# A last projection in half-width strips, and both halves of a query projection in one PSUM bank, in a two-part decode kernel

## The chip, the cores and the metric

One core of a Trainium2 chip. The metric is the device time of one execution in microseconds (us). The span is what the profile records, from the first to the last instruction; the timed number is 1.7 to 2.3 us more.

## The reference

Two attention layers decode one token, and their outputs are put side by side.

```
A: q = x @ wq                      x 1x512, wq 512x4096, 32 heads of 128
   p = softmax(q k^T / sqrt(128))  k, v: 32 heads x 32768 keys x 128, bf16
   a = (p v, heads side by side) @ wo        wo 4096x512
B: the same with 8 key/value heads, 4 query heads to each, last 4096 keys only
out = [a, b]                       1 x 1 x 1024
```

A alone reads 512 MiB of keys and values. The arithmetic is small beside that.

## The kernel before

SyncE queues loads deep ahead of their use. After the first query projection come B's attention, then 32 heads of A. The weights of the last projection, B's wo in two pieces and A's in five that shrink toward the end, are queued behind the last keys and values. So what follows the last byte is the rest of A's last projection and the store.

The query projection fills two banks, four strips of 512 in each:

```python
banks = (self.ACC, self.PT)
for tt in range(4):
    for b in range(2):
        for c in range(STRIPS):
            w = 4096 * tt + 512 * (4 * b + c)
            e.matmul(banks[b][32 * c:32 * c + 1, :], lhsT=t["x"][:, tt:tt + 1], rhs=wq[:, w:w + 512],
                     start=(tt == 0), stop=(tt == 3), tile_position=(0, 32 * c), ...)
# ... each bank cast to qrow by VectorE, then 8 small matmuls turn the rows into columns
```

The last projection: heads go in fours to four 32-column tiles of the array. B's pieces, and A's first three (heads 0 to 24), make four partial rows. VectorE copies these 128 partitions, and a float32 matmul with a column of ones folds them into two half rows. Then A's heads 25 to 31 are added in two half-width strips.

```python
WO_CUTS = {"A": (0, 11, 19, 25, 29, 32), "B": (0, 16, 32)}

def halves(self, e, bank, lhsT, rhs, begin, end):
    for i in range(2):
        e.matmul(bank[64 * i:64 * i + 1, 0:256], lhsT=lhsT, rhs=rhs[:, 256 * i:256 * i + 256],
                 start=begin, stop=end, tile_position=(0, 64 * i), ...)

for name, cut, bank, to in (("B", 2, self.S, self.ACC), ("A", 3, self.T[1], self.PT)):
    ...
    for part in range(cut):                      # four strips: bank[32 * (a % 4)]
        o = self.proj_part(name, part, ...)
    strips = dve(tensor_copy(self.pb[:, :], bank[:, :]), o, free)
    o = free = pe(self.halves(e, to, self.e32[:, 0:1], self.pb, True, whole), strips, ...)
    if whole:
        self.store("B", self.ACC, 512, o)
for part in range(3, 5):
    o = self.proj_part("A", part, ... self.halves(e, self.PT, lhsT, rhs, False, a == 31))
self.store("A", self.PT, 0, o)                   # cast, then a 1 KB store
```

## Time and profile before

| | before |
|---|---|
| time, median of the first 3 runs (range) | 1327.97 us (1327.24 to 1328.51) |
| the profiled run: time, span | 1328.94, 1327.2 us |
| DMA | 570.6 MB, 430 GB/s, one queue 99.6% of 16 engines' span |
| A's last wo piece lands | 1289.2 (issue) + 33.4 = 1322.6 us |
| from that landing to the end | 4.6 us |

From the page of the kernel before: TensorE's busy share and instructions, then busy tenths in 40 slices of the span, the granted TensorE clock in tenths of full speed, DMA, and the load queue's row.

```profile
PE 970.6 (73%) x13239; PEld 677.0 (51%) x13239; DVE 753.9 (57%) x1351; ACT 54.8 (4%) x167; POOL 2.2 (0%) x17
...
PEclk8886888887878888787888878788887878888797
DMA  9999999999999999999999999999999999999997
...
q1 hardware_dynamic: 13192, 570.44, 99.6%
```

No compute engine is full; DMA is. Only its last slice is thinner, and that slice holds the tail.

The chain of waits of the kernel before, its end: start, length, what.

```profile
1288.23 32.18 DMA kbuf<-in_A_wo_dram
1320.41 0.04 issue
1320.45 1.03 PE psT L742 x6
1321.48 0.02 issue
1321.51 0.70 DVE pb L745
1322.21 0.04 issue
1322.25 2.53 PE psPT L725 x18
1324.78 0.02 issue
1324.80 0.42 DVE out_sb L731
```

The last load in the chain is the third wo piece, not the fifth. The copy and the fold hold up the 14 matmuls of the last two pieces, which landed meanwhile. The matmuls of the tail in the timeline (start, length, operation, count, and in brackets the idle time before it and what ended it):

```profile
1316.06 0.81 PE L742 MATMUL psT<-kbuf,oz_A 128*1 128x512 bf16 x11 [1.13 <-DMA kbuf<-in_A_wo_dram]
1318.56 1.02 PE L742 MATMUL psT<-kbuf,oz_A 128*1 128x512 bf16 x8 [1.69 <-DMA kbuf<-in_A_wo_dram]
1320.45 1.02 PE L742 MATMUL psT<-kbuf,oz_A 128*1 128x512 bf16 x6 [0.87 <-DMA kbuf<-in_A_wo_dram]
...
1322.25 1.02 PE L725 MATMUL psPT<-pb,e 128*1 128x256 f32 x4 [0.79 <-DVE pb L745]
1323.06 1.71 PE L725 MATMUL psPT<-kbuf,oz_A 128*1 128x256 bf16 x14
```

Eleven matmuls took 0.81 us, the next eight 1.02 us. The windows view of the same stretch says why. Its columns are the stretch, its length, each engine's busy time (and count), and at the end the granted clock, the DMA share and GB/s.

```profile
1316.00:1318.00 2.00, 0.81 (x11) 0.19 (x11) 0.00 (x0) 0.00 (x0) 0.00 (x0) 0.87 1.00 411
1318.00:1320.00 2.00, 1.02 (x8) 0.10 (x8) 0.00 (x0) 0.00 (x0) 0.00 (x0) 0.50 0.99 390
1320.00:1322.00 2.00, 1.02 (x6) 0.10 (x6) 0.49 (x1) 0.00 (x0) 0.00 (x0) 0.50 0.42 149
1322.00:1324.00 2.00, 1.75 (x14) 0.85 (x16) 0.20 (x1) 0.00 (x0) 0.00 (x0) 0.50 0.01 0
```

The clock is at half from about 1317.5 us to the end of the work.

### The profile page before, as it was taken

What the parts mean: (1) busy time and instruction counts of PE and PEld (TensorE: products, weight loads), DVE (VectorE), ACT (ScalarE), POOL (GpSimd) and SP (SyncE); (2) the same over time, 40 slices, a digit from 0 to 9 for tenths busy, and PEclk for the clock granted to TensorE, in tenths of its full rate; (3) what the DMA queues carried; (4) which work ended last, traced back from release to release, by engine and by line L of the source; (5) the groups of instructions that cost most, each with busy time, mean ns of one, the idle gap of its engine ahead of it and who ended that gap; (6) DMA issues with size and microseconds to landing.
All of it is one profiled execution on the core that took longest, in us unless ns stands there. A gap on an engine that the chain in (4) does not pass through costs nothing. (4 is left out here: it accounts for less than half of the span.)

```text
span 1327.2 us, 28802 instructions
## 1 busy us (share of the span) xinstructions
PE 970.6 (73%) x13239; PEld 677.0 (51%) x13239; DVE 753.9 (57%) x1351; ACT 54.8 (4%) x167; POOL 2.2 (0%) x17
## 2 busy tenths in 40 slices
PE   4675678777777877767787776768777676877785
PEld 3463446555444655544465554446555444655552
DVE  4663556664555666455566645556664555666562
ACT  0000000000000000000000000000000000000000
POOL 0000000000000000000000000000000000000000
PEclk8886888887878888787888878788887878888797
DMA  9999999999999999999999999999999999999997
GB/s 402 429 436 426 442 429 440 427 440 431 425 440 431 440 427 438 433 429 437 433 440 425 440 431 429 438 431 440 425 438 433 429 437 433 440 425 438 433 429 330
DMA packets 13492, 570.60 MB, mean 430 GB/s; under 512 B 1828, under 2 KB 1832, under 8 KB 2216
## 3 DMA queue, kind: packets, MB, share of 16 engines
q1 hardware_dynamic: 13192, 570.44, 99.6%
q8 instruction: 8, 0.13, 0.0%
q10 hardware_dynamic: 288, 0.00, 0.0%
q14 instruction: 4, 0.03, 0.0%
HBM read 570.43 MB, written 0.00 MB: 430 GB/s over the span
## 5 line engine op out<-in xcount | busy, mean ns | idle before, releaser
L564 DVE COPY kt<-psT 128x1024 bf16<-128x1024 bf16 x1056 | 655.6, 683 | 235.7 <-PE psT L560 234.3
L560 PE MATMUL psT<-ident,kbuf 128*128 128x128 bf16 x8448 | 581.4, 235 | 165.4 <-DMA kbuf<-in_A_k_cache_dram 152.4
L560 PEld LDWEIGHTS psT<-ident,kbuf 128*128 128x128 bf16 x8448 | 541.8, 106 | 257.7 <-DMA kbuf<-in_A_k_cache_dram 160.5
L663 PE MATMUL psACC<-vbuf,ptsb 128*4 128x512 bf16 (+1 forms) x2112 | 187.6, 532 | 22.8 <-ACT ptsb L638 22.0
L583 PE MATMUL psS<-kt,qw 128*32 128x512 bf16 x2048 | 157.6, 385 | 14.9 <-DVE kt L564 14.9
L677 DVE TENSOR_SCALAR oc_A<-psACC,hot_A 128x128 f32<-128x128 f32 x32 | 11.2, 350 | 252.5 <-PE psG L690 252.5
L663 PEld LDWEIGHTS psACC<-vbuf,ptsb 128*4 128x4 bf16 (+1 forms) x2112 | 60.7, 111 | 140.1 <-issue 93.6
L611 ACT ACTIVATE psb<-psS,nb_A 128x512 bf16<-128x512 f32 x32 | 22.0, 687 | 1167.9 <-DVE nb_A L610 1167.9
L583 PEld LDWEIGHTS psS<-kt,qw 128*32 128x32 bf16 x2048 | 34.0, 95 | 57.6 <-DVE kt L564 30.7
L690 PE MATMUL psG<-oc_A,hw 128*32 128x128 f32 (+1 forms) x128 | 19.3, 227 | 52.3 <-DVE oc_A L679 52.3
L690 PEld LDWEIGHTS psG<-oc_A,hw 128*32 128x32 f32 x128 | 11.4, 109 | 62.4 <-DVE oc_A L679 55.0
L635 PE MATMUL psPT<-ident,psb 128*128 128x128 bf16 x136 | 18.3, 279 | 34.0 <-ACT psb L611 34.0
L679 DVE SCALAR_TENSOR_TENSOR oc_A<-psACC,hot_A,oc_A 128x128 f32<-128x128 f32 x96 | 33.6, 350 | 3.4
L600 DVE TENSOR_REDUCE tr_in<-psS 128x1 f32<-128x512 f32 x34 | 23.5, 692 | 17.1 <-PE psS L583 17.1
L635 PEld LDWEIGHTS psPT<-ident,psb 128*128 128x128 bf16 x136 | 10.4, 119 | 37.1 <-ACT psb L611 36.7
L604 PE MATMUL psACC<-rows,tr_in 128*1 128x64 f32 x64 | 8.7, 217 | 25.6 <-DVE tr_in L600 25.6
L638 ACT ACTIVATE ptsb<-psPT 128x512 bf16<-128x512 bf16 x34 | 20.3, 597 | 30.6 <-PE psPT L635 30.6
L604 PEld LDWEIGHTS psACC<-rows,tr_in 128*1 128x1 f32 x64 | 2.7, 81 | 35.1 <-DVE tr_in L600 35.1
L608 PE MATMUL psACC<-mr_A,nscale 1*128 1x1 f32 x64 | 12.1, 256 | 9.7 <-DVE mr_A L607 9.7
L608 PEld LDWEIGHTS psACC<-mr_A,nscale 1*128 1x128 f32 x64 | 9.4, 182 | 15.7 <-DVE mr_A L607 15.7
L610 DVE COPY nb_A<-psACC 128x1 f32<-128x1 f32 x32 | 5.1, 158 | 15.0 <-PE psACC L608 15.0
L607 DVE TENSOR_REDUCE mr_A<-psACC 1x1 f32<-1x64 f32 x32 | 6.8, 213 | 11.7 <-PE psACC L604 11.7
(85 smaller groups left out, 74.8 us busy)
## 6 DMA issues: line engine op xcount, KB each, us to landing
kbuf<-in_A_k_cache_dram SPq DMA_DIRECT2D x4, 4096.0 KB, 22.6
kbuf<-in_B_k_cache_dram SPq DMA_DIRECT2D x2, 4096.0 KB, 32.0
vbuf<-in_B_v_cache_dram SPq DMA_DIRECT2D x2, 4096.0 KB, 25.0
vbuf<-in_B_wq_dram SPq DMA_DIRECT2D x1, 4096.0 KB, 12.6
vbuf<-in_A_wq_dram SPq DMA_DIRECT2D x1, 4096.0 KB, 32.2
kbuf<-in_B_wo_dram SPq DMA_DIRECT2D x2, 2048.0 KB, 33.4
kbuf<-in_A_wo_dram SPq DMA_DIRECT2D x1, 1408.0 KB, 28.6
kbuf<-in_A_wo_dram SPq DMA_DIRECT2D x1, 1024.0 KB, 30.8
```

The lines of the kernel that those rows point to most:

```text
L560: inst = e.transpose(T[:, 128 * k:128 * k + 128], src[:, DH * k:DH * k + DH], self.ident[:, :])
L564: self.copies.append(self.op("dve", lambda v: v.tensor_copy(KT[:, :], T[:, :]), o, to="pe"))
L583: inst = e.matmul(self.S[32 * c:32 * c + 32, :], lhsT=win, rhs=self.kt[(bb + c // 2) % NKT][:, 512 * (c % 2):512 * (c % 2) + 512], start=b ...
L600: o = dve(lambda v: v.reduce_max(tr["in"][:, 0:1], self.S[:, :], axis=AXX), self.sdone, self.k_pool, to="pe" if name == "A" else None)
L604: o = self.op("pe", lambda e: e.matmul(self.ACC[0:1, 0:64], lhsT=tr["in"][:, 0:1], rhs=self.rows64[:, :], start=True, stop=True, skip_grou ...
L608: o = self.op("pe", lambda e: e.matmul(self.ACC[:, 64:65], lhsT=self.nscale[:, :], rhs=t["mr"][0:1, :], start=True, stop=True, skip_group_ ...
L611: self.sread = self.op("act", lambda s: s.activation(out=self.psb[:, :], in_=self.S[:, :], func=ACTF.Exp, bias=t["nb"][:, k:k + 1], scale= ...
L635: inst = e.transpose(PT[:, 128 * jj:128 * jj + 128], self.psb[:, 128 * jj:128 * jj + 128], self.ident[:, :])
L638: self.ptread = self.op("act", lambda s: s.activation(out=self.ptsb[:, :], in_=PT[:, 0:512], func=ACTF.Copy), self.psread, to="pe")
L663: inst = e.matmul(acc[32 * c:32 * c + rows, 0:512], lhsT=lhsT, rhs=rhs, start=begin, stop=end, tile_position=(0, 32 * c), skip_group_check ...
L679: o = self.op("dve", lambda v, src=src, hot=hot: v.scalar_tensor_tensor(out=oc, in0=src, scalar=hot, in1=oc, op0=ALU.mult, op1=ALU.add), p ...
L690: return self.op("pe", lambda e: e.matmul(self.G[0:32, c0 + c:c0 + c2], lhsT=win, rhs=t["oc"][g % len(t["oc"])][:, c:c2], start=False, sto ...
```

## The change

Its intent: take the copy and the fold off the end of A's projection, and take VectorE work out of the start. Three parts:

1. A's first wo piece (11 heads) runs as one full-width row. It is copied and folded in while later pieces land. Pieces 1 to 4 go straight into two half-width strips. B's rows are folded by one full-width float32 matmul.
2. Both halves of the query projection share one bank: x is stored between zeros, so a two-column window of it puts a half in row 0 or row 1 of a strip. One cast instead of two, four turning matmuls instead of eight.
3. Fewer VectorE steps for constants: some are built on GpSimd, four copies become one, one memset goes.

```diff
-                x=sb(f"x_{name}", [128, 4], BF16),
+                x=sb(f"x_{name}", [128, 12], BF16),
 ... (query projection)
+                    x = t["x"][:, 4 - 4 * b + tt:9 - 4 * b + tt:4]
-                        inst = e.matmul(banks[b][32 * c:32 * c + 1, :], lhsT=t["x"][:, tt:tt + 1], rhs=wq[:, w:w + 512],
-                                        start=(tt == 0), stop=(tt == 3), ...
+                        inst = e.matmul(acc[32 * c:32 * c + 2, :], lhsT=x, rhs=wq[:, w:w + 512], start=(tt == 0 and b == 0),
+                                        stop=(tt == 3 and b == 1), ...
-        for b in range(2):
-            o = self.op("dve", lambda v, b=b: v.tensor_copy(self.qrow[:, 512 * b:512 * b + 512], banks[b][:, :]), o)
+        self.accread = o = self.op("dve", lambda v: v.tensor_copy(self.qrow[:, :], acc[:, :]), o)
 ... (last projection; the old loop shown above is removed)
+        rows = o = self.op("pe", lambda e: e.matmul(self.ACC[0:1, :], lhsT=self.e32[:, 0:1], rhs=self.pb[:, :], ...
 ... (B's row is cast to qrow and stored)
+        row = self.proj_part("A", 0, lambda e, lhsT, rhs, a: e.matmul(
+            self.T[1][0:1, :], lhsT=lhsT, rhs=rhs, start=(a == 0), stop=(a == top - 1), ...))
+        row = self.op("dve", lambda v: v.tensor_copy(self.pb[0:1, :], self.T[1][0:1, :]), row, rows)
+        for part in range(1, len(self.WO_CUTS["A"]) - 1):
+            if part == 3:
+                self.op("pe", lambda e: self.halves(e, self.PT, self.e32[0:1, 0:1], self.pb[0:1, :], False, False), row)
+            o = self.proj_part("A", part, lambda e, lhsT, rhs, a: self.halves(e, self.PT, lhsT, rhs, a == top, a == 31))
 ... (constants, buffer shapes and the store's buffer left out)
```

More of the change, by code (lines that the diff above doesn't have):

```diff
@@ L277, in alloc @@
         self.e32 = sb("e32", [128, 32], F32)
-        self.spread = sb("spread", [32, 4, 128], BF16)
+        self.spread = sb("spread", [32, 4 * 129], BF16)
         self.tr = {k: sb(f"tr_{k}", [128, 32], F32) for k in ("in", "a")}
@@ L283, in alloc @@
         self.pb = sb("pb", [128, 512], F32)
-        self.out_sb = sb("out_sb", [128, 512], BF16)
+        self.out_sb = sb("out_sb", [128, 256], BF16)
         self.marks = sb("marks", [16, 17 * 16], BF16)
@@ L305, in alloc @@
         self.qa = sb("qa", [128, NQH], BF16)
-        self.qrow = sb("qrow", [128, 1024], BF16)
+        self.qrow = sb("qrow", [128, 512], BF16)
         self.qw = sb("qw", [128, 64], BF16)
@@ L454, in constants @@
         pool(lambda g: g.memset(self.qw[:, :], 0.0))
-        pool(lambda g: g.memset(self.spread[:, :, :], 0.0))
-        pool(lambda g: g.memset(self.rows64[:, :], 0.0))
+        pool(lambda g: g.memset(self.spread[:, :], 0.0))
+        for n in ("B", "A"):
+            for i in (0, 8):
+                self.k_x = pool(lambda g, n=n, i=i: g.memset(c[n]["x"][:, i:i + 4], 0.0))
+        rows = pool(lambda g: g.memset(self.rows64[:, :], 1.0))
+        pool(lambda g: g.affine_select(
+            out=self.rows64[:, :].rearrange("p (s r) -> p s r", r=16), in_=self.rows64[:, :].rearrange("p (s r) -> p s r", r=16),
+            pattern=[[-32, 4], [-1, 16]], compare_op=ALU.is_equal, fill=0.0, base=0, channel_multiplier=1), rows)
         pool(lambda g: g.memset(self.nscale[:, :], -self.SCALE))
@@ L463, in constants @@
         dve(lambda v: v.memset(self.G[:, :], 0.0))
-        dve(lambda v: v.memset(self.PT[:, :], 0.0))
         self.accread = dve(lambda v: v.memset(self.ACC[:, :], 0.0))
@@ L467, in constants @@
             self.op("act", lambda e, n=n: e.dma_start(
-                c[n]["x"][:, :], self.X[n]["x"][0, 0, :].rearrange("(p t) -> p t", t=4)).then_inc(self.xsem[n], 16))
+                c[n]["x"][:, 4:8], self.X[n]["x"][0, 0, :].rearrange("(p t) -> p t", t=4)).then_inc(self.xsem[n], 16))
         for s in range(STRIPS):
@@ L479, in constants @@
             dve(lambda v, t=t, HG=HG: v.tensor_copy(t["hsel"][:, 32:32 + HG], t["lh"][:, :]), lh, self.k_pool)
-        for s in range(STRIPS):
-            rows = slice(32 * s, 32 * s + 32)
-            dve(lambda v, rows=rows, s=s: v.tensor_copy(self.rows64[rows, 16 * s:16 * s + 16],
-                                                        self.ident[rows, 32 * s:32 * s + 16]), self.k_pool)
-        for dq in range(4):
-            self.k_sel = dve(lambda v, dq=dq: v.tensor_copy(self.spread[:, dq, dq:128:4], self.ident[0:32, 0:32]),
-                             self.k_pool)
+        self.k_sel = dve(lambda v: v.tensor_copy(
+            self.spread[:, :].rearrange("p (a b) -> p a b", b=129)[:, :, 0:125:4],
+            self.ident[0:32, 0:32].unsqueeze(1).to_broadcast([32, 4, 32])), self.k_pool)
     def emit_qproj(self, name):
@@ L491, in emit_qproj @@
         slot = self.WQ_SLOT[name]
-        wq = self.vbuf[:, HALF * DH * slot:HALF * DH * (slot + 1)]
-        banks = (self.ACC, self.PT)
+        wq, acc = self.vbuf[:, HALF * DH * slot:HALF * DH * (slot + 1)], self.ACC
         def mm(e):
@@ L497, in mm @@
                 for b in range(2):
+                    x = t["x"][:, 4 - 4 * b + tt:9 - 4 * b + tt:4]
                     for c in range(STRIPS):
                         w = 4096 * tt + 512 * (4 * b + c)
-                        inst = e.matmul(banks[b][32 * c:32 * c + 1, :], lhsT=t["x"][:, tt:tt + 1], rhs=wq[:, w:w + 512],
-                                        start=(tt == 0), stop=(tt == 3), tile_position=(0, 32 * c), skip_group_check=True)
+                        inst = e.matmul(acc[32 * c:32 * c + 2, :], lhsT=x, rhs=wq[:, w:w + 512], start=(tt == 0 and b == 0),
+                                        stop=(tt == 3 and b == 1), tile_position=(0, 32 * c), skip_group_check=True)
             return inst
-        o = self.op("pe", mm, (self.xsem[name], 16), self.landed("v", slot), self.accread, self.qread, to="dve")
+        o = self.op("pe", mm, (self.xsem[name], 16), self.landed("v", slot), self.accread, self.qread, self.k_x, to="dve")
         self.free["v"][slot] = o
-        for b in range(2):
-            o = self.op("dve", lambda v, b=b: v.tensor_copy(self.qrow[:, 512 * b:512 * b + 512], banks[b][:, :]), o)
-        self.accread = o
+        self.accread = o = self.op("dve", lambda v: v.tensor_copy(self.qrow[:, :], acc[:, :]), o)
         ps = self.G[:, 400:432]
@@ L510, in turn @@
             inst = None
-            for b in range(2):
-                for i in range(4):
-                    inst = e.matmul(ps[:, 16 * b + i:16 * b + i + 13:4], lhsT=self.qrow[:, 512 * b + 128 * i:512 * b + 128 * i + 128],
-                                    rhs=self.ident[:, 0:97:32], start=True, stop=True, skip_group_check=True)
+            for i in range(4):
+                inst = e.matmul(ps[:, i:i + 29:4], lhsT=self.qrow[:, 128 * i:128 * i + 128],
+                                rhs=self.ident[:, :].rearrange("p (c r) -> p r c", r=32)[:, 0:2, :],
+                                start=True, stop=True, skip_group_check=True)
             return inst
@@ L704, in mm @@
             for dq in range(4):
-                inst = e.matmul(p2[:, 0:32], lhsT=self.spread[:, dq, :], rhs=t["ob"][:, 32 * dq:32 * dq + 32],
+                inst = e.matmul(p2[:, 0:32], lhsT=self.spread[:, 128 * dq:128 * dq + 128], rhs=t["ob"][:, 32 * dq:32 * dq + 32],
                                 start=(dq == 0), stop=(dq == 3), skip_group_check=True)
@@ L729, in store @@
     def store(self, name, bank, off, dep):
-        c = slice(off // 2, off // 2 + 256)
-        o = self.op("dve", lambda v: v.tensor_copy(self.out_sb[0:65, c], bank[0:65, 0:256]), dep)
+        o = self.op("dve", lambda v: v.tensor_copy(self.out_sb[0:65, :], bank[0:65, 0:256]), dep)
         self.op("sp", lambda e: e.dma_start(self.out[0, :, off:off + 512].rearrange("a (i x) -> (a i) x", i=2),
-                                            self.out_sb[0:65:64, c]).then_inc(self.outsem[name], 16), o)
+                                            self.out_sb[0:65:64, :]).then_inc(self.outsem[name], 16), o)
@@ L735, in emit_proj @@
     def emit_proj(self):
-        free = None
-        for name, cut, bank, to in (("B", 2, self.S, self.ACC), ("A", 3, self.T[1], self.PT)):
-            whole = name == "B"
-            top = self.WO_CUTS[name][cut]
-            for part in range(cut):
-                o = self.proj_part(name, part, lambda e, lhsT, rhs, a, bank=bank, top=top: e.matmul(
-                    bank[32 * (a % 4):32 * (a % 4) + 1, :], lhsT=lhsT, rhs=rhs, start=(a < 4), stop=(a >= top - 4),
-                    tile_position=(0, 32 * (a % 4)), skip_group_check=True))
-            strips = self.op("dve", lambda v, bank=bank: v.tensor_copy(self.pb[:, :], bank[:, :]), o, free)
-            o = free = self.op("pe", lambda e, to=to, whole=whole: self.halves(e, to, self.e32[:, 0:1], self.pb, True, whole),
-                               strips, self.accread)
-            if whole:
-                self.store("B", self.ACC, 512, o)
@@ L750, in emit_proj @@
-        for part in range(3, len(self.WO_CUTS["A"]) - 1):
-            o = self.proj_part("A", part, lambda e, lhsT, rhs, a: self.halves(e, self.PT, lhsT, rhs, False, a == 31))
+        top = self.WO_CUTS["A"][1]
+        for part in range(len(self.WO_CUTS["B"]) - 1):
+            o = self.proj_part("B", part, lambda e, lhsT, rhs, a: e.matmul(
+                self.S[32 * (a % 4):32 * (a % 4) + 1, :], lhsT=lhsT, rhs=rhs, start=(a < 4), stop=(a >= 28),
+                tile_position=(0, 32 * (a % 4)), skip_group_check=True))
@@ new lines, in emit_proj @@
+        strips = self.op("dve", lambda v: v.tensor_copy(self.pb[:, :], self.S[:, :]), o)
+        rows = o = self.op("pe", lambda e: e.matmul(self.ACC[0:1, :], lhsT=self.e32[:, 0:1], rhs=self.pb[:, :], start=True,
+                                             stop=True, skip_group_check=True), strips, self.accread)
+        o = self.op("dve", lambda v: v.tensor_copy(self.qrow[0:1, :], self.ACC[0:1, :]), o)
+        self.op("sp", lambda e: e.dma_start(self.out[0, :, 512:1024], self.qrow[0:1, :]).then_inc(self.outsem["B"], 16), o)
@@ new lines, in emit_proj @@
+        row = self.proj_part("A", 0, lambda e, lhsT, rhs, a: e.matmul(
+            self.T[1][0:1, :], lhsT=lhsT, rhs=rhs, start=(a == 0), stop=(a == top - 1), skip_group_check=True))
+        row = self.op("dve", lambda v: v.tensor_copy(self.pb[0:1, :], self.T[1][0:1, :]), row, rows)
[3 more added lines that the diff above has]
+            o = self.proj_part("A", part, lambda e, lhsT, rhs, a: self.halves(e, self.PT, lhsT, rhs, a == top, a == 31))
```

## The prediction

> **What bounds the kernel.** The DMA. The profile's queue table gives one queue 99.6% of 16 engines' span, 570.6 MB at a mean of 430 GB/s; in the slices DMA is at 9 tenths in 39 of 40. PE is busy 73%, DVE 57%; neither limits. So the time is start-up, plus a stream of bytes that the change leaves alone, plus what follows the last byte. The chain of waits ends in A's wo load, 6 projection matmuls (1.03 us), the strip copy (0.70), 18 matmuls (2.53), the output cast (0.42), and the store to the end at 1327.2.
>
> **Front.** The query projection fills one bank instead of two. Its 32 matmuls per input stay (groups of four at 0.21 us at full clock); one 0.69 us DVE cast and half of the 8 small turning matmuls go: 0.75 to 0.9 us per projection. The constants lose one 0.48 us memset and six or seven DVE copies of 0.11 to 0.18 us; POOL gains a few. None is on the critical path: the first matmul waits until 13.49 us for x_B (load unchanged), DVE constants end at 5.75 us, and later the DMA queue holds several MB (loads land 20 to 30 us after issue). The transposes wait for DMA both times. Worth: 0.
>
> **Tail.** Landings, by issue plus issue-to-landing: A's five wo pieces at about 1316.0, 1318.5, 1320.4, 1321.65 and 1322.6 us. Before, PE could not end soon after 1322.6, for the strips were folded late: third piece at 1320.45, copy, float32 fold at 1322.25 (0.81 us), then 14 half-width matmuls (1.71), all at half clock: PEclk falls to 0.50 at 1317.45. PE ends at 1324.78.
> After, piece 0 (11 heads) runs as one row, about 11 x 0.215 = 2.4 us instead of 0.81, while piece 1 lands; pieces 1 to 4 run as pairs of half strips. At full clock a pair is 0.107 us: piece 1 0.9, piece 2 0.65, fold 0.4, piece 3 0.45; each ends near the next landing. After the last landing only 3 heads remain, 0.35 us plus 0.17 to drain: PE ends near 1323.15. Cast and store stay, so the gain is 1.3 to 1.6 us.
> Will the clock hold? The Trainium skill, "TensorE: Matmul & The Clock Gate", Part 1, gives a free-running window of about 3.4 us that sets full or half clock. This trace agrees: the clock changes at 1300.4, 1307.25 and 1317.45, two and three windows apart. My estimate: windows busy 41 to 44% went cold, one of 52% stayed warm. After the change they should be 65 to 70% busy (the longer piece 0, and B's full-width float32 fold of about 1 us instead of 0.60), so warm. If the clock halves at 1317.4 again, piece 0 ends at 1319.7, backlog builds, and PE ends at about 1325: no gain.
>
> **Predicted: 1326.5 us**, 1324.9 to 1328.0 at 8 in 10. Faster by over 2%: 0.005; within 2%: 0.99; slower: 0.005.
>
> **What would show it.** Chain: last wo piece, 6 half-width matmuls (under 0.7 us), cast, store, no strip copy; PE waiting for DMA before the wo pieces; PEclk 1.0 to 1320 or later; DMA rate unchanged; qproj's cast once per input, the next transposes still waiting for DMA.
>
> **What would make it wrong.** Half clock during piece 0; single-row matmuls spaced wider than 0.215 us by their weight loads; a shift of DMA bandwidth between runs (0.1% is as large as the gain; the three runs spread over 1.27 us).

## The result, and the profile after

The changed kernel took 1327.23 us (median of 6, 1327.03 to 1329.22); the kernel before took 1327.86 us (median of 6, 1326.98 to 1328.51). The ratio is 0.9999, with a 95% interval of 0.9986 to 1.0011: the same. Ratios here are made from fast runs; they are not quite the ratios of the medians.

The profiled spans tell another story: 1327.2 us before, 1324.9 us after, 2.3 us less. Both statements are correct, and the experiments are about how they fit together.

The clock, DMA and queue rows of the page, for the changed kernel:

```profile
PEclk8886788887878888787888878788887879887898
DMA  9999999999999999999999999999999999999998
...
q1 hardware_dynamic: 13190, 570.44, 99.7%
```

The end of its chain of waits:

```profile
1288.99 32.85 DMA kbuf<-in_A_wo_dram
1321.85 0.04 issue
1321.89 0.51 PE psPT L724 x6
1322.40 0.02 issue
1322.42 0.42 DVE out_sb L729
```

It is the predicted chain: the fifth wo piece, six matmuls (predicted 0.35 + 0.17, measured 0.51), cast, store. From landing to the end are 3.05 us instead of 4.6. In the timeline of the changed kernel each piece waits for its load and ends before the next is there:

```profile
1315.32 2.54 PE L745 MATMUL psT<-kbuf,oz_A 128*1 128x512 bf16 x11 [0.21 <-DMA kbuf<-in_A_wo_dram]
...
1317.82 1.04 PE L724 MATMUL psPT<-kbuf,oz_A 128*1 128x256 bf16 x16
...
1319.70 0.82 PE L724 MATMUL psPT<-kbuf,oz_A 128*1 128x256 bf16 x12 [0.84 <-DMA kbuf<-in_A_wo_dram]
1320.45 0.59 PE L724 MATMUL psPT<-pb,e 1*1 1x256 f32 x4
1320.97 0.60 PE L724 MATMUL psPT<-kbuf,oz_A 128*1 128x256 bf16 x8
1321.89 0.49 PE L724 MATMUL psPT<-kbuf,oz_A 128*1 128x256 bf16 x6 [0.32 <-DMA kbuf<-in_A_wo_dram]
```

Eight heads in half strips took 1.04 us: sixteen matmuls, eight pairs of 0.107 us and some 0.17 us to drain (the eleven full-width rows before them took 2.54 us, 0.215 us each and the same drain; by that, one half-width matmul alone takes an estimated 0.107 us). The Trainium skill, "TensorE: Matmul & The Clock Gate", Part 3, has matmuls in different column tiles run at once; this trace agrees, since one at a time sixteen of 0.107 us would need 1.7 us. The clock in the windows view of the changed kernel:

```profile
1316.00:1318.00 2.00, 2.00 (x13) 0.72 (x13) 0.11 (x1) 0.00 (x0) 0.00 (x0) 1.00 0.99 409
1318.00:1320.00 2.00, 1.16 (x22) 0.70 (x20) 0.57 (x1) 0.00 (x0) 0.00 (x0) 1.00 0.98 381
```

It stays full. The last landing, 1321.85 against 1322.6 us, is earlier by 0.75 us; nothing in the change moves loads, and over all the profiles below the last landing lies between 1321.85 and 1322.6 us with either kernel. So, between these two profiles, 1.55 of the 2.3 us are the tail and 0.75 us are how the stream happened to run.

### The profile page after: what moved, and what is told of

Its sections match the earlier page's. It is cut to its first block, busy times and chain, and to the rows that moved or that the text cites. A ratio compares the mean times of both kernels' runs of the same rounds, so it can differ in the third digit from the quotient of the medians.

```text
span 1324.9 us, 28805 instructions
## 1 busy us (share of the span) xinstructions
PE 966.8 (73%) x13243; PEld 673.9 (51%) x13243; DVE 751.2 (57%) x1341; ACT 54.8 (4%) x167; POOL 2.6 (0%) x22
```

## The experiments

The times beside the labels are of each kernel's own runs; 27 runs of the kernel before were made beside them. "Landing" is the landing of A's last wo piece, worked out as issue plus issue-to-landing.

### e1_after_again: the changed kernel, once more

No edit.

> The changed kernel once more, five rounds, to narrow the interval. My theory: from the landing of A's last wo piece to the end of the span the kernel before needs 4.6 us (landing at 1322.6, end 1327.2) and the changed one 3.05 us (landing at 1321.85, end 1324.9), so 1.55 us (0.12%) is gained; the rest of the 2.3 us between the two profiled spans is a stream of loads that happened to be 0.75 us quicker. Expect a ratio of 0.9988 with the interval possibly touching 1, and a profile with 3.0 to 3.1 us from landing to end. Rival (the tail gain is an accident of one profile, nothing is gained): landing to end over 4 us in this profile, or a ratio of 1.000.

Measured: median 1327.36 us (1327.04 to 1327.97), ratio 0.9999 (0.9985 to 1.0012). In the profile, landing at 1322.1, end at 1325.2: 3.1 us. The short tail is no accident of one profile. But here it has no slack: the attention ended later than in the first profile of the changed kernel (B's projection began at 1313.51 instead of 1311.39 us), and from B's fold at 1316.21 us on the chain of waits stays on TensorE, through the long first piece (2.27 us), and reaches the last piece at 1322.18 us, just after it landed. Yet the ratio did not move: it is above the expected 0.9988. The runs of the kernel before explain the interval. They were not spread evenly: 1326.70, 1326.76, 1327.03 and 1327.07, then nothing, then five from 1328.39 to 1328.67. (The six of the first comparison don't split so cleanly: 1326.98, 1327.24, 1327.75, 1327.97, 1328.40 and 1328.51.)

### e2_tail_only: the new last projection alone

The kernel before with the changed last projection, everything else as before.

> The new last projection alone; the query projections and constants stay as before. My theory (all of the gain is in the tail): landing of the last wo piece to the end 3.0 to 3.1 us, as in the changed kernel, ratio to before about 0.9988. Rival (the front gives something, for instance by issuing loads earlier): a ratio nearer 1 than that of the changed kernel by 0.0005 or more, and the last landing later by over 0.7 us.

Measured: 1327.06 us (1326.89 to 1327.24), ratio 0.9995 (0.9981 to 1.0009); landing 1322.2, end 1325.3: 3.1 us. The short tail comes with this part alone. No run is in the upper group. The ratio, as in e1, is above the expected 0.9988.

### e3_front_only: the new front alone

The changed kernel with the old last projection.

> The new query projections and constants alone; the last projection stays as before. My theory: VectorE has 1.5 to 2.5 us less work before 40 us and that is worth nothing: ratio 1.000 (within 0.0007), landing of the last wo piece to the end 4.4 to 4.8 us, the transposes at about 22.5 and 43.4 us still wait for their load. Rival (the front is worth about 1 us): ratio 0.9993 or less with a last landing earlier by 0.7 us or more.

Measured: 1327.62 us (1326.87 to 1328.71), ratio 0.9999 (0.9986 to 1.0013). The profiled run, 1328.64 us, has landing 1321.9, end 1326.5: 4.6 us, and half clock. The old tail is back; two of the five runs are in the upper group, the others at 1326.87, 1327.24 and 1327.62 us. The front's gain turned into waiting, which the waits of the first 60 us show (engine, tile and line, what it waited for: us in total, times, longest). First the kernel before:

```profile
PE psT L560 <- DMA kbuf<-in_B_k_cache_dram: 9.2, 2, 5.4
```

and the changed kernel:

```profile
PE psT L559 <- DMA kbuf<-in_B_k_cache_dram: 11.0, 2, 6.2
```

VectorE's busy time in those 60 us fell from 33.42 to 31.23 us, and TensorE waits 1.8 us longer for keys.

### e4_tail_heavy: a known cost on the tail

```diff
-        o = self.op("dve", lambda v: v.tensor_copy(self.out_sb[0:65, :], bank[0:65, 0:256]), dep)
+        for _ in range(13):
+            o = dep = self.op("dve", lambda v: v.tensor_copy(self.out_sb[0:65, :], bank[0:65, 0:256]), dep)
```

> The changed kernel with the output cast done 13 times instead of once, for both sizes the same work: a known cost of 12 x 0.38 to 0.43 = 4.6 to 5.2 us on the chain after the last load. My theory: it shows one for one, landing to end about 7.6 to 8.2 us, and the time is 4.6 to 5.2 us over that of the changed kernel (ratio to before 1.0023 to 1.0028): the timing can see microseconds of the tail. Rival (the end of the span overlaps something else, so that tail time is not device time): less than 2.5 us more.

Measured: 1332.48 us (1332.43 to 1332.58), ratio 1.0036 (1.0022 to 1.0050); landing 1322.2, end 1330.7: 8.5 us. The thirteen casts took 5.87 us, so 5.45 us were added, a little more than I had expected since each repeat costs 0.45 us. The mean span rose by 5.3 us over the changed kernel's (1330.74 against 1325.45 us, mean of its 11 runs). So microseconds of the tail show in the span one for one. The mean time rose by less, 4.9 us (1332.49 against 1327.55 us): within the expected 4.6 to 5.2 us and far from the rival's 2.5, but some 0.35 us less than the span did; this comes up again below. The expected ratio, 1.0023 to 1.0028, was missed, because it took the changed kernel to be 0.12% faster than the kernel before.

### e5_old_tail_busy: the old tail with TensorE kept busy

The grouping called for a second theory: the groups are the granted clock in the tail. The edit is against the kernel before.

```diff
+                if name == "A":
+                    self.idle_work((7, 6, 0)[part])    # that many full-width matmuls into a bank nobody reads
```

> The kernel before, with 7 and 6 full-width matmuls without a use (into a bank that nobody reads) after A's first and second wo piece, so that TensorE stays busy while it waits for loads. The first twelve timed runs on record and those of this study show the kernel before in two groups: 1326.7 to 1327.1 us and 1328.4 to 1328.7 us. My new theory: the groups are the granted TensorE clock in the last 6 us (the two profiled runs with the old last projection, at 1328.9 and 1328.6 us, have it at half from 1317 us). Then this kernel has no run of the upper group: all five at 1326.5 to 1327.3 us, the profile shows PEclk 1.0 to 1322 us, and landing to end 3.0 to 3.3 us although the schedule is the old one. Rival A (the groups come from the stream of loads): two groups here as well. Rival B (the half-width strips themselves are the gain): landing to end stays over 4 us, times up to 1328.5 us.

Measured: 1327.89 us (1327.23 to 1327.98); landing 1322.1, end 1326.3: 4.2 us, at full clock. None of the five runs is in the upper group, as the theory said, but the lower was not reached: my numbers for it failed, and a tail of over 4 us is what rival B had foretold. The end of this kernel's chain of waits:

```profile
1320.81 0.42 PE psT L740 x2
1321.23 0.45 PE psT L753 x2
1321.70 0.70 DVE pb L758
...
1322.45 1.38 PE psPT L725 x18
1323.85 0.42 DVE out_sb L731
```

In this run the attention ended 2.4 us later than in the profile of before, so TensorE had no idle time to fill, and the matmuls without a use (L740) pushed the copy to 1321.70. The fold and the 14 matmuls after it took 1.38 us, against 2.53 us at half clock. So the test had a cost of its own, and the full clock of this run need not be its work: in e9, below, the kernel before keeps full clock without it when its attention ends late. It does not settle the matter.

### e6_new_tail_idle: the new order with TensorE as idle as before

The new order of pieces 1 to 4, but with piece 0 in four strips (0.81 us instead of 2.54 us) and B's fold in halves, on the front of before. The cut shows the lines that differ from the changed kernel's.

```diff
-        row = self.proj_part("A", 0, lambda e, lhsT, rhs, a: e.matmul(self.T[1][0:1, :], ...))
-        row = self.op("dve", lambda v: v.tensor_copy(self.pb[0:1, :], self.T[1][0:1, :]), row, rows)
+        row = self.strips4("A", 0, self.T[1], top)
+        row = self.op("dve", lambda v: v.tensor_copy(self.pb[:, :], self.T[1][:, :]), row, rows)
```

> The kernel before with the new order of A's last projection (pieces 1 to 4 in half-width strips, the first piece folded in before piece 3), but the first piece in four strips at once and B's fold in halves, as before, so that TensorE is as idle around 1316 us as in the kernel before. My theory: the clock falls to half near 1317 us in some runs, in which the PE ends about 0.5 to 1.1 us later after the landing than in the changed kernel (landing to end 3.5 to 4.2 us), and in runs at full clock it takes 3.0 to 3.1 us; times from 1326.8 to 1328.2 us, spread over 0.7 us. Rival B (the order of the work is the whole gain, the clock is nothing): landing to end 3.0 to 3.1 us at either clock and times no more spread than the changed kernel's.

Measured: 1326.98 us (1326.67 to 1327.31), ratio 0.9992 (0.9978 to 1.0005); landing 1322.3, end 1325.3: 3.0 us. The windows view of this run, cut where its clock changes:

```profile
1314.69:1318.10 3.41, 1.41 (x15) 0.28 (x15) 1.28 (x3) 0.00 (x0) 0.00 (x0) 1.00 1.00 411
1318.10:1321.51 3.41, 3.22 (x30) 1.72 (x32) 0.00 (x0) 0.00 (x0) 0.00 (x0) 0.50 0.79 303
```

The clock did fall to half at 1318.10, as I expected; it cost nothing, as I did not. At half clock pieces 1 and 2 took so long that TensorE was busy 3.22 of 3.41 us, and at 1321.51, just before the last landing, the clock came back. For this one run rival B is right: the order of the work keeps the tail short, and the clock was not needed.

### e7, e8, e9 and e10: the kernel before, four more looks

No edit; the question was what the lower group looks like inside.

> The kernel before, unchanged, for a second profile. If its time is in the lower group (1326.7 to 1327.1 us): my theory expects PEclk at 1.0 to the end and landing to end about 3.2 us; the rival (stream of loads) expects half clock and 4.6 us with a last landing near 1321 us. If it is in the upper group: half clock and 4.6 us again, which tells nothing apart.

> The same once more, since one execution falls in either group with about even chances: lower group with PEclk 1.0 to the end and landing to end about 3.2 us, upper group with PEclk 0.5 from about 1317 us and landing to end about 4.6 us. The rival (stream of loads) expects the clock and the landing-to-end time to have nothing to do with the group.

> The kernel before, a further profile, in search of its lower group. The profiles so far show two phases: either the PV matmuls of head 30 and the first transposes of head 31 run at full clock (wo issued at 1287 to 1288 us, attention over early, TensorE idle near 1316 us, then half clock), or at half clock (wo issued at 1289 to 1290 us, attention over 2 us later, TensorE full to the end at full clock). My theory: the upper group of the kernel before is the first phase, with landing to end 4.4 to 4.7 us; the lower group is the second, with landing to end 3.0 to 3.4 us. Rival (the group comes from the stream of loads alone): a profile in the lower group with landing to end over 4.2 us and a last landing before 1321.2 us.

> As the look before it: in the first phase (wo issued by 1288.3 us) half clock after 1317 us, landing to end 4.4 to 4.7 us, time 1328.3 to 1328.9 us; in the second phase (wo issued after 1289 us) full clock to 1322 us, landing to end 3.0 to 3.4 us, time 1326.6 to 1327.2 us.

| look | time | landing | end | landing to end | clock after 1318.5 us |
|---|---|---|---|---|---|
| e7_before_look | 1328.68 | 1322.4 | 1326.9 | 4.5 | 0.5 |
| e8_before_look2 | 1328.78 | 1322.4 | 1327.0 | 4.6 | 0.5 |
| e9_before_look3 | 1326.85 | 1322.1 | 1325.1 | 3.0 | 1.0 |
| e10_before_look4 | 1328.89 | 1322.6 | 1327.2 | 4.6 | 0.5 |

The third look caught the lower group; the fourth, on the same chip, is in the upper one, and each has the clock, the tail and the time that were expected of it beforehand. They were run on another chip. The chain of waits of the third, the same kernel as in the profile before:

```profile
1289.82 30.07 DMA kbuf<-in_A_wo_dram
...
1319.93 0.62 PE psT L742 x6
...
1320.57 0.70 DVE pb L745
...
1321.31 1.38 PE psPT L725 x18
...
1322.71 0.42 DVE out_sb L731
```

From the third piece's landing to the end of the matmuls it is 2.81 us here and 4.37 us in the profile before. The two matmul entries give the whole difference: 1.03 - 0.62 = 0.41 and 2.53 - 1.38 = 1.15, together 1.56 us. Everything else in the chain is alike. So the old tail costs no more than the new one when the clock is full; its extra 1.5 us are half-clock matmuls. Together with e6 this makes four cases of landing to end: old order at half clock 4.6 us, old order at full clock 3.0, new order at full clock 3.05, new order with one half-clock window 3.0. Only the first is long. The second and the fourth rest on one profile each. The rival, a stream of loads that runs early, is out: the landing in the lower run is within 0.5 us of the others, and its landing to end is 1.5 us shorter.

Why the clock differs: cut into windows of 3.41 us where the clock changes, the window that decided is, in the kernel before (profile of before):

```profile
1314.04:1317.46 3.42, 1.41 (x15) 0.28 (x15) 0.65 (x2) 0.00 (x0) 0.00 (x0) 1.00 0.99 408
```

in the lower look (e9):

```profile
1315.54:1318.95 3.41, 1.85 (x23) 0.50 (x23) 0.55 (x2) 0.00 (x0) 0.00 (x0) 1.00 1.00 406
```

and in the changed kernel:

```profile
1313.68:1317.09 3.41, 2.79 (x11) 0.80 (x12) 1.03 (x2) 0.00 (x0) 0.00 (x0) 1.00 0.97 405
```

TensorE was busy 41% of the first, and the clock was halved at its end; it was busy 54% of the second and 82% of the third, and the clock held. (54% is close to the edge: see the last section.) The lower look differs in two things: where the windows lie, and that the attention of head 31 ended 1.4 us later than in the profile of before, so B's projection, its fold and A's first piece lie closer together. The later attention comes from the windows as well. In the lower look the last but one head's 64 PV matmuls (probabilities times values) took 6.02 us and the next head's first 64 transposes 5.02 us; in the profile of before they took 4.95 and 3.82 us. The clock there was at half up to 1274.58 and from 1277.99 to 1281.40 us in the lower look, and full from 1273.09 to 1300.40 us in the profile of before. Where the windows fall at the start of an execution is chance as far as these runs show.

### e11_front_heavy: more work in the front

```diff
-        self.accread = o = self.op("dve", lambda v: v.tensor_copy(self.qrow[:, :], acc[:, :]), o)
+        for _ in range(9):
+            o = self.op("dve", lambda v: v.tensor_copy(self.qrow[:, :], acc[:, :]), o)
+        self.accread = o
```

> The changed kernel with the cast of each query projection done nine times: 8 x 0.73 = 5.8 us more VectorE work on each of the two projections, eight times what the change took away. My theory (the front is off the path, loads are queued 20 us deep): the time stays within 0.5 us of the changed kernel's (1327.0 to 1327.9 us, ratio 0.999 to 1.000); unit B1's transposes still wait for their load near 43.4 us; those of B0 start up to 2 us later than 22.5 us. Rival (the front is on the path): 5 to 12 us more.

Measured: 1327.04 us (1326.91 to 1327.10, 4 runs); end of span 1325.2. It was run on another chip. Each projection's nine casts took 6.49 us instead of 0.69, and the time did not rise. B's first transposes began at 23.63 us, 1.1 us later, and those of the second load still waited 0.8 us of weight-load time for it. The chain of waits still ends in the last wo piece and six matmuls of 0.51 us.

5.8 us more at either place did not show in the time: the front is off the path.

### e12_last_one: a smaller last load

The kernel of the sixth experiment with one head in the last piece.

```diff
-    WO_CUTS = {"A": (0, 11, 19, 25, 29, 32), "B": (0, 16, 32)}
+    WO_CUTS = {"A": (0, 11, 19, 25, 29, 31, 32), "B": (0, 16, 32)}
```

> The new last projection of the sixth experiment (the quickest so far, 1326.98 us) with A's last load cut in two, so that one head instead of three comes last. Theory: two of three pairs of matmuls leave the end, 2 x 0.107 us, so landing to end 2.8 us instead of 3.0 us and a time about 0.2 us lower, 1326.8 us, if the smaller last load (1 KB pieces) lands no later. Rival: the additional load costs as much as it saves, landing later by 0.2 us or more; time equal or above 1327 us. Either is below what the timing can tell for sure; the profile is to say which.

Measured: 1327.09 us (1326.76 to 1327.38), mean span 1325.26 us against 1325.14 us without it (e6, on the other chip). In the profile, landing to end is 2.8 us, as expected (landing 1322.1, end 1324.9), but the time did not fall. What it saves is below what these runs resolve.

## Why the prediction was right, and where it was off

**The class and the range were right.** With DMA busy for 99.6% of the span and a change that touches no load, there was no room for a gain of 2%. 1327.23 us lies in the stated 1324.9 to 1328.0. That says little: the median of the kernel before, 1327.86 us, lies in it too.

**"Front. Worth: 0" was right.** The saved VectorE time went into a longer wait for keys (9.2 to 11.0 us), and 5.8 us more work on each projection cost nothing (e11).

**The tail's mechanism was right.** "PE ends near 1323.15" was 0.55 us after the expected landing; measured, it was 0.55 us after the landing, in the chain that was described, at full clock, with the busy shares of the windows at 82% and 75%, above the predicted 65 to 70%. (One share in the prediction was misread: of the windows that ended in half clock in the profile of before, one is 41% busy and the other, 1296.98 to 1300.40 us, 47%, not 44%.)

**The size was off: "the gain is 1.3 to 1.6 us".** That is the difference to a tail at half clock, and the prediction took it off the median of before. But the profile of before was of a run of 1328.94 us, above all three timed runs. Of the 27 runs of before, 13 took over 1328.2 us (mean 1328.52) and ten took under 1327.2 us (mean 1326.92); four lie between, from 1327.36 to 1327.74 us, and were not profiled. Four of the five profiles of before, all over 1328.6 us, have the half-clock tail; the one at 1326.85 us has the full clock and already ends 3.0 us after the landing. There the change has nothing to gain. On the average of the spans, 1326.03 us for those 27 and 1325.45 us for 11 of the changed kernel, the gain is 0.6 us, not 1.5 (95% interval, worked out from the spread of these runs: 0.1 to 1.1). The step that failed is the silent one, that the profiled tail is the tail of every run.

**A second loss was not foreseen.** In all 11 listed runs of the changed kernel the time is 2.05 to 2.14 us over the span, in the 27 of before 1.69 to 1.81 us. So some 0.35 us of the 0.6 us were given back outside the profile: the mean times are 1327.78 and 1327.55 us, 0.2 us apart, which is not clear of the spread (-0.3 to 0.7). e3, with the new front alone, has 2.07 to 2.14 us too. Yet e4 and e11, which contain that front and a dozen or more further casts, have 1.71 to 1.80 us. And e2, e5, e6 and e12, which have the old front, go from 1.68 to 2.31 us, from run to run of one kernel. So it is not the front's work. One thing in the profiles goes with it: the queue q14, of the kind "instruction" on the page, has 3 packets in the three profiles of the kernels with the constant 2.1 us (changed kernel, e1, e3) and 4 in the eleven others. A last load of instructions that falls behind the end of the span would fit; no run tests it, and it does not explain the spread in e5. The cause stays open.

**Also open.** One of the 11 runs of the changed kernel took 1329.22 us with a span of 1327.1 us. It was not profiled. The prediction's case of a clock that halves while the long first piece runs would look like that, but nothing shows it. In e6 the clock halved and the new order lost nothing, with a first piece of 0.81 us. Whether the long first piece of the changed kernel is as safe was not seen; in e1 it left no slack at full clock.

**A better version?** By their means e6 (1326.95 us), e11 (1327.02), e2 and e12 (both 1327.09) were quicker than the changed kernel (1327.55 us); that e11, which only adds work to it, is among them shows how little such differences mean. e6 needs neither the long first piece nor the new front. But no interval except that of e4 excludes 1, so that e6 beats the others is not shown.

## What to carry to other kernels

Compare a profile's own time with the timed runs before you subtract from it: if the runs fall into groups, the profile shows one of them, and a gain measured against it may belong to that group alone. In a tail where TensorE waits for loads, its clock can decide how long the work after the last load takes (here 4.6 us instead of 3.0); an order that leaves only the last load's work after the last load is short at full clock, and in the one half-clock window seen here too. Saving work in front of a stream that was queued 20 us deep only lengthened a wait.

## What the Trainium skill lacked or had wrong

- "TensorE: Matmul & The Clock Gate", Part 1, has a free-running window of about 3.4 us and two clock states; all profiles here agree (windows of 3.41 us, clock 0.5 or 1.0). It calls the windows idle or busy without saying how busy. Here, by the profile's modelled busy time, windows of 41% near the end ended in half clock and windows of 54% and 61% kept full clock; near 50% it went either way (48% kept it in e5, 50% lost it in e9, and so did 53% early in e9, 1.82 of 3.41 us from 96.98 us). To come back was harder: at half clock, windows of 77% (2.62 of 3.41 us, kernel before, 1320.87 to 1324.28 us) and 80% (2.72 us, e5, 1268.88 to 1272.29 us) did not bring the full clock back, windows of 79% (2.70 us, e9, 1277.99 to 1281.40 us) and 94% (e6) did.
- The same page, "Why this matters for your kernels", asks for no idle gaps over about 3 us. In the kernel before the largest wait of the matmuls in the window that ended in half clock was 1.13 us; the next, of 1.69 us, began in it and ended after it. Short gaps that add up to 59% of a window were enough.
- The same page says that the place of the window varies from run to run and puts the cost of the ramp at the start under 1% of a typical span. What was lost here is not that ramp but a half-clock tail, 1.6 us of 1328 (0.12%), as small; but it is larger than the whole gain of this change, and, as far as five profiles show, it makes the two groups among the runs of one kernel (means 1326.92 and 1328.52 us), which the page does not say.
- "DMA: Bandwidth & Descriptors", the section on the anatomy of one DMA, fits a fixed cost of about 2.0 us to transfers issued by GpSimd. Here a 1 KB store issued by SyncE took 2.0 us from its issue (1322.87 us) to the end of the span (1324.9 us): about the same figure for a transfer that another engine issued.
- No page says that what the timed number has over the profile's span can differ between two kernels, or between the runs of one: here its mean is 2.10 us for the changed kernel and 1.75 us for the kernel before, and 1.68 to 2.31 us within the five runs of e5.
